# Last tokens of k and v on 128 partitions, token sums placed in VectorE's gaps, and another order of sigmoids, in a fused linear-attention and GEGLU kernel

## The chip, the cores and the metric

The kernel runs on one core of a Trainium2 chip. The metric is the device time of one execution in microseconds (us). Executions were timed on the chip, several for each kernel, and medians with their ranges are given. "Before" is the kernel as it was, "after" is the kernel with the whole change.

Names: PE is TensorE (matrix products), DVE is VectorE, ACT is ScalarE, POOL is GpSimd, SP is SyncE, which here only issues transfers. A letter q behind an engine's name is its sequencer. "Full clock" means that the throttle grants PE its full frequency.

## The reference, cut to what matters

```python
def _attn_ref(q, k, v, g_norm):            # q, k, v: (8 batches, 8 heads, 576 tokens, 64)
    kv  = np.einsum('bhsd,bhse->bhde', k, v)
    out = np.einsum('bhsd,bhde->bhse', q, kv)
    rms = np.sqrt(np.mean(out * out, axis=-1, keepdims=True) + 1e-06)
    return (out / rms * g_norm)

def _moe_ref(x, w_gate, w_val, w_out, w_res):   # x: 4608 tokens x 512, d_ff 1536
    g = x @ w_gate
    val = x @ w_val
    ffn_out = gelu(g) * val @ w_out              # (shortened)
    res_gate = 1.0 / (1.0 + np.exp(-(x @ w_res)))
    return x + res_gate * ffn_out
```

k^T v over all 576 tokens of a head has to be there before anything else can start: nothing of a batch's output exists without its last tokens.

## The kernel before

The tokens are worked on in nine blocks of 512. Blocks 0 to 7 hold the first 512 tokens of each batch, with four tokens (j = 0..3) of one head group on each partition; block 8 holds the 64 last tokens of every batch. Three places matter.

**The opening.** Batch 0's q, k and v come in halves (four heads first, then two head pairs one after the other), issued by SP. Its 64 last tokens of k and v are loaded apart, on 32 partitions with two tokens each, into tiles whose other 96 partitions are set to zero, so that their product may use all 128 rows:

```python
def load_first_last(half):
    hs = slice(half * HH, (half + 1) * HH)                    # four heads
    for i, t in enumerate((k, v)):
        nc.sync.dma_start(
            out=first_raw[i][half][0 : R // 2, :].rearrange("p (h x) -> p h x", h=HH),
            in_=t[0, hs, M0:S, :].rearrange("h (p j) d -> p h (j d)", j=2),
        )
...
for which, t in (("q", q), ("k", k), ("v", v)):
    load_first(which, t, 0, HH)
    if which == "k":
        load_first_last(0)
for pr in range(NP // 2, NP):                                 # head pairs 2 and 3
    load_first("q", q, 2 * pr, 2 * pr + 2)
    load_first("k", k, 2 * pr, 2 * pr + 2)
    if pr == NP // 2:
        load_first_last(1)
    load_first("v", v, 2 * pr, 2 * pr + 2)
...
def f_kv(pr):
    ...
    for j in range(NJ):
        nc.tensor.matmul(ps, lhsT=k16[:, j, cs], rhs=b16_t[0, "v"][:, hs, j * D : (j + 1) * D], ...)
    for j in range(2):
        kl, vl = (t[:, j].rearrange("p h d -> p (h d)")[:, cs] for t in first_last)
        nc.tensor.matmul(ps, lhsT=kl, rhs=vl, start=False, stop=(j == 1))
```

**The end of an ordinary block** (blocks 6 and 7 are the ones concerned). The output product is made of seven products of half size; bank A is written, read by DVE and written again. `rest` carries additions of tokens that the next block needs (`ts`):

```python
prod(w["A"], s_[1], wo_t[:, 1], False)
sub(nc.vector, w["F"], w["A"], w["d"], ALU.add)
prod(w["E"], a_of(blk, 1, 2), b_of(2, 1), False)
pf((0, 0), w["E"])
for f in rest:                       # all four token sums
    f()
prod(w["A"], s_[2], wo_t[:, 2], False)
c22 = res_all[part((1, 1))]
sub(nc.vector, c22, w["A"], w["d"], ALU.add)     # bank A is free only after this
prod(w["F"], s_[3], b_of(2, 2), False)
...
prod(w["A"], a_of(blk, 2, 2), wo_t[:, 3], False)
```

**The last block** makes its four sigmoids on ACT after two copies, in the order 2, 3, 0, 1; POOL then forms `u` from sigmoids 2 and 3, and DVE adds `u` near the end.

## Time and profile before

| | |
|---|---|
| time, median of the timed executions beside the change | 343.72 us (343.55 to 343.92, 4 runs) |
| the profiled execution | 348.22 us, of which 346.3 us from first to last instruction |
| busy: PE, DVE, ACT, POOL | 95%, 75%, 47%, 32% of that span |
| first product of the regular part (the first gps with four products in a row) | 27.31 us |

The page of the kernel before opens with these lines; the digits are the busy share in tenths, in 40 equal slices of the span:

```profile
span 346.3 us, 6525 instructions
...
PE   8779999999999999999999999999999899989992
```

PE is filled nearly everywhere. It is not in the first three slices (26 us: the opening), in two or three slices late in the run (the ends of blocks 6 and 7), and in the last (the tail). These are the places that the change touches. In the prediction and below, lines of the chain of waits read "start, duration, what", and lines of a timeline "start, duration, engine, line, operation, out<-in, shape, how often", with the idle time before it and its cause in brackets.

### The profile page before, as it was taken

The numbers are of one execution on the slowest core, as the hardware profiler recorded it, in microseconds if no ns is written. First come the engines' busy times: TensorE is split into PE (matmuls) and PEld (weight loads), VectorE is DVE, ScalarE is ACT, GpSimd is POOL, SyncE is SP. The second block draws the span as 40 slices with busy tenths as digits, with TensorE's granted clock in tenths as the row PEclk, the third lists the DMA queues.
The fourth block names the chain that finished last, engine by engine and source line by source line (L and its number), as shares of the span: only waits on it lengthen the run. The fifth ranks groups of instructions, "written<-read, shape, count | busy, mean of one in ns | idle before, by whom it ended". The sixth has DMA issues, their size and how long they took to land.

```text
span 346.3 us, 6525 instructions
## 1 busy us (share of the span) xinstructions
PE 330.3 (95%) x2576; PEld 202.9 (59%) x2576; DVE 258.3 (75%) x498; ACT 161.3 (47%) x289; POOL 110.1 (32%) x127
## 2 busy tenths in 40 slices
PE   8779999999999999999999999999999899989992
PEld 3534454444854476447644674466546778778882
DVE  5474529749958988878677978796799787677854
ACT  3355365454526361536163525353544366636750
POOL 2692160892043207400650066005000431151222
PEclk9999999999999999999999999999999999999999
DMA  7999999359389363983498349935103030011004
GB/s 242 281 182 204 194 203 169 86 132 182 44 148 180 122 77 107 188 94 70 140 172 87 61 123 178 105 61 139 62 0 61 2 137 2 2 51 73 0 2 121
DMA packets 76688, 38.82 MB, mean 112 GB/s; under 512 B 42098, under 2 KB 74354, under 8 KB 76658
## 3 DMA queue, kind: packets, MB, share of 16 engines
q0 software_dynamic: 38752, 17.17, 39.5%
q1 hardware_dynamic: 37328, 20.71, 22.0%
q10 hardware_dynamic: 578, 0.52, 0.4%
q8 instruction: 20, 0.33, 0.4%
q14 instruction: 10, 0.08, 0.1%
HBM read 38.80 MB, written 9.44 MB: 139 GB/s over the span
## 4 chain that ended last, share of the span: by engine, by line
PE 86%; DVE 7%; DMA 2%; ACT 2%; issue 1%; SPq 1%; DVEq 0%
PE gps L357 21%; PE vps L357 20%; PE wA L452 9%; PE rps L377 8%; PE Av L682 3%; PE Ag L682 3%; PE fps L394 3%; PE wD L452 3%; PE w L452 2%; DMA hid_s<-in_v_dram 2%; PE wF L452 2%; PE wE L452 2%; PE kvp L208 2%; PE Fv L682 2%; PE Fg L682 2%; DVE ts L425 1%
## 5 line engine op out<-in xcount | busy, mean ns | idle before, releaser
L345 ACT ACTIVATE ge<-gps 128x512 f16<-128x512 f32 x84 | 50.0, 597 | 98.5 <-PE gps L357 97.7
L357 PE MATMUL vps<-xT,wv 128*128 128x512 f16 x328 | 84.2, 379 | 0.8 <-DVE hid L346 0.8
L357 PE MATMUL gps<-xT,wg 128*128 128x512 f16 x328 | 84.3, 380 | 0.0
L346 DVE TENSOR_TENSOR hid<-ge,vps 128x512 f16<-128x512 f16 x84 | 57.4, 684 | 32.6 <-PE vps L357 28.7
L488 POOL TENSOR_TENSOR osb<-osb,t 128x512 f32<-128x512 f32 x28 | 36.2, 1311 | 138.9 <-DVE osb L484 133.1
L357 PEld LDWEIGHTS <-wv 128*128 128x128 f16 x328 | 32.1, 98 | 39.7 <-issue 1.1
L357 PEld LDWEIGHTS <-wg 128*128 128x128 f16 x328 | 30.7, 98 | 34.5 <-issue 0.2
L452 PEld LDWEIGHTS <-hid_s 128*128 128x128 f16 x384 | 37.6, 98 | 4.5 <-issue 0.2
L452 PEld LDWEIGHTS <-hid 128*128 128x128 f16 x288 | 28.1, 98 | 8.2 <-issue 3.5
L377 PE MATMUL rps<-wr,xT 128*128 128x512 f16 x144 | 32.5, 379 | 0.0
L386 ACT ACTIVATE th<-rps 128x512 f32<-128x512 f32 x36 | 21.5, 597 | 16.4 <-PE rps L377 16.4
L377 PEld LDWEIGHTS <-xT 128*128 128x128 f16 x144 | 14.1, 98 | 16.6
L245 DVE TENSOR_REDUCE ss<-sq 128x8 f32<-128x512 f32 x32 | 20.6, 680 | 2.9 <-ACT sq L243 2.7
L682 PEld LDWEIGHTS <-ws 128*128 128x128 f16 x192 | 18.8, 98 | 3.3 <-issue 1.2
L452 PE MATMUL wA<-wo_ts,hid_s 128*128 128x256 f16 x168 | 20.6, 273 | 0.0
L391 ACT ACTIVATE th<-th 128x512 f32<-128x512 f32 x36 | 19.8, 622 | 0.0
L303 DVE TENSOR_TENSOR t<-op,ny 128x512 f16<-128x512 f32 x28 | 17.9, 683 | 0.1
L243 ACT ACTIVATE sq<-op 128x512 f32<-128x512 f32 x28 | 15.3, 596 | 4.5 <-PE op L226 4.2
L317 DVE TENSOR_TENSOR t<-t,g 128x512 f16<-128x512 f16 x36 | 16.2, 500 | 0.1
L425 DVE TENSOR_TENSOR hid_s<-hid 128x1536 f16<-128x1536 f16 x16 | 15.3, 954 | 0.2
L719 POOL TENSOR_TENSOR hid<-ge,c 128x512 f16<-128x512 f16 x6 | 7.0, 1164 | 25.6 <-ACT ge L713 25.6
L452 PE MATMUL wA<-wo_ts,hid 128*128 128x256 f16 x84 | 10.3, 272 | 2.3 <-DVE osb L425 2.3
(172 smaller groups left out, 481.4 us busy)
## 6 DMA issues: line engine op xcount, KB each, us to landing
out_dram<-osb SPq DMA_DIRECT2D x14, 512.0 KB, 2.6
qraw<-in_q_dram POOLq DMA_DIRECT2D x7, 512.0 KB, 7.8
k<-in_k_dram POOLq DMA_DIRECT2D x7, 512.0 KB, 9.5
v<-in_v_dram POOLq DMA_DIRECT2D x7, 512.0 KB, 11.3
wg<-in_moe_w_gate_dram POOLq DMA_DIRECT2D x2, 512.0 KB, 8.6
wv<-in_moe_w_val_dram POOLq DMA_DIRECT2D x2, 512.0 KB, 9.4
wo<-in_moe_w_out_dram POOLq DMA_DIRECT2D x2, 512.0 KB, 14.2
out_dram<-osb SPq DMA_DIRECT2D x4, 256.0 KB, 2.8
```

What stands on the lines that cost most here:

```text
L245: nc.vector.tensor_reduce(out=out_, in_=sq, op=ALU.add, axis=mybir.AxisListType.X)
L303: nc.vector.tensor_tensor(out=t, in0=o, in1=scale, op=ALU.mult)
L345: nc.scalar.activation(out=ge, in_=gps, func=AF.Gelu)
L346: nc.vector.tensor_tensor(out=hids[blk][:, f, :], in0=ge, in1=vps, op=ALU.mult)
L357: nc.tensor.matmul(ps[:, j0 * P : j1 * P], lhsT=w[:, cc, :], rhs=xT_t[blk][:, j0:j1, cc, :], start=(cc == 0 and j0 == 0), stop=(cc == NP - ...
L377: nc.tensor.matmul(rps, lhsT=xT_t[blk][:, j, cc, :], rhs=wr16[:, cc, :], start=(cc == 0), stop=(cc == NP - 1),)
L386: nc.scalar.activation(out=th, in_=rps, func=AF.Tanh, scale=0.5)
L391: nc.scalar.activation(out=th, in_=th, func=AF.Copy, scale=0.5, bias=0.5)
L425: eng.tensor_tensor(out=out_, in0=in0, in1=in1, op=op)
L452: nc.tensor.matmul(ps[:, e - es[0], :], lhsT=a[:, f, e * P : (e + 1) * P], rhs=b[:, f, :], start=(start and e == es[0] and f == 0), stop=( ...
L488: nc.gpsimd.tensor_tensor(out=res_all[of], in0=res_all[of], in1=t_t[blk][of], op=ALU.add)
L682: nc.tensor.matmul(out_[:, r, :], lhsT=lhsT, rhs=rhs, start=(first and r == 0 and c == 0), stop=(c == 1), skip_group_check=True,)
```

## The change

Its intent: give the last tokens of batch 0 all 128 partitions (four heads of 32 rows each), so that loads and casts are short and no zeros are needed; place each token sum on its own in a gap of DVE, and the last tokens' normalisation in an earlier gap; start two sigmoids earlier in the last block. Cut to its core:

```diff
@@ the opening
-        first_last.append(t[:, 2 * H * NJ * D :][:, 0 : 2 * H * D].rearrange("p (j h d) -> p j h d", j=2, h=H))
-        first_raw.append([th_all[:, 2 * len(first_raw) + i, :] for i in range(2)])
+        first_last.append(t[:, 2 * H * NJ * D :][:, 0 : 4 * D].rearrange("p (i j d) -> p i j d", i=2, j=2))
+        first_raw.append([th_all[:, 2 * len(first_raw) + i, 0 : 2 * D] for i in range(2)])
...
-                out=first_raw[i][half][0 : R // 2, :].rearrange("p (h x) -> p h x", h=HH),
-                in_=t[0, hs, M0:S, :].rearrange("h (p j) d -> p h (j d)", j=2),
+                out=first_raw[i][half],
+                in_=t[0, hs, M0:S, :].rearrange("h (p j) d -> h p (j d)", j=2),
...
-    for t in first_last:
-        nc.vector.memset(t, 0.0)
...
+        for j in range(NJ - 1):
+            whole(j)                      # 128 rows, as before
         for j in range(2):
-            kl, vl = (t[:, j].rearrange("p h d -> p (h d)")[:, cs] for t in first_last)
-            nc.tensor.matmul(ps, lhsT=kl, rhs=vl, start=False, stop=(j == 1))
+            for e in range(2):            # 32 rows, one head
+                i = 2 * (pr % 2) + e
+                kl, vl = (t[i * R // 2 : (i + 1) * R // 2, pr // 2, j, :] for t in first_last)
+                nc.tensor.matmul(ps[halves(e), halves(e)], lhsT=kl, rhs=vl, start=False, stop=False)
+        whole(NJ - 1)
@@ the end of blocks 6 and 7
             prod(w["A"], s_[1], wo_t[:, 1], False)
+            aside("F")                    # the last tokens' normalisation (block 6)
             sub(nc.vector, w["F"], w["A"], w["d"], ALU.add)
+            aside("00")                   # one token sum
             prod(w["E"], a_of(blk, 1, 2), b_of(2, 1), False)
             pf((0, 0), w["E"])
-            for f in rest:
-                f()
+            aside("22")                   # one token sum
             prod(w["A"], s_[2], wo_t[:, 2], False)
             c22 = res_all[part((1, 1))]
             sub(nc.vector, c22, w["A"], w["d"], ALU.add)
+            aside("01")                   # one token sum
             prod(w["F"], s_[3], b_of(2, 2), False)
             ...
+            aside("11")                   # one token sum
@@ the last block
                 prod(wa[e], a_of(blk, 1, 1), b_of(1, 1), True, (e,))
+            for j in (2, 3):
+                m_sigmoid(j)
+            for e in range(2):
                 nc.scalar.copy(out=we[:, one[e], :], in_=wa[e])
             ...
-            for j in (2, 3, 0, 1):
+            for j in (0, 1):
                 m_sigmoid(j)
```

More of the change, by code (lines that the diff above doesn't have):

```diff
@@ L459, in prod, with out_by_products, aside @@
                 )
-    def out_by_products(blk, later, banks, rest=()):
+    def out_by_products(blk, later, banks, amid):
         w = {}
         s_ = hid_sums
+        def aside(ahead_of):
+            for f in amid.get(ahead_of, ()):
+                f()
         def res(jj):
@@ L870, in f_cast_last @@
     def f_cast_last(i, half, copy):
-        hs = slice(half * HH, (half + 1) * HH)
-        copy(
-            out=first_last[i].rearrange("p j h d -> p h j d")[0 : R // 2, hs, :, :],
-            in_=first_raw[i][half][0 : R // 2, :].rearrange("p (h j d) -> p h j d", h=HH, j=2),
-        )
+        copy(out=first_last[i][:, half], in_=first_raw[i][half].rearrange("p (j d) -> p j d", j=2))
     def f_qT(pr):
@@ L890, in f_kv, with whole @@
         hs, cs = of_pair(pr)
-        for j in range(NJ):
+        def whole(j):
             nc.tensor.matmul(
-                ps, lhsT=k16[:, j, cs], rhs=b16_t[0, "v"][:, hs, j * D : (j + 1) * D], start=(j == 0), stop=False
-            )
+                ps,
+                lhsT=k16[:, j, cs],
+                rhs=b16_t[0, "v"][:, hs, j * D : (j + 1) * D],
+                start=(j == 0),
+                stop=(j == NJ - 1),
+            )
+        for j in range(NJ - 1):
+            whole(j)
         for j in range(2):
-            kl, vl = (t[:, j].rearrange("p h d -> p (h d)")[:, cs] for t in first_last)
-            nc.tensor.matmul(ps, lhsT=kl, rhs=vl, start=False, stop=(j == 1))
+            for e in range(2):
[3 more added lines that the diff above has]
+        whole(NJ - 1)
     def f_kv_out(pr):
@@ L1084, in plan_attn @@
             if b == 3:
-                amid_out[m - 1] = [lambda: by_token(b), *begin]
+                amid_out[m - 1] = {"22": [lambda: by_token(b), *begin]}
             else:
@@ L1102, in plan_attn @@
             at(m, NF if b == 2 and j > 1 else n0 + j // 2, lambda j=j: a_t(b, j))
-        if rem:
-            at(m, NF + 3, lambda: a_t(b, NJ))
         for j in range(NJ):
@@ L1107, in plan_attn @@
         at(m, NF, lambda: d_xT(b, 0, NJ))
-        if rem:
-            at(m, NF + 3, lambda: a_x(b, NJ), lambda: d_xT(b, NJ, NJ + 1))
+        last = [lambda: a_t(b, NJ), lambda: a_x(b, NJ), lambda: d_xT(b, NJ, NJ + 1)]
+        if rem and b + 1 == B:
+            amid_out.setdefault(m, {})["F"] = last
+        elif rem:
+            at(m, NF + 3, *last)
     units = [(n, g) for g in range(NF // GF) for n in "gv"]
@@ L1170 @@
             if blk + 1 in LAST:
-                amid_out.setdefault(blk, []).extend(token_sums(blk + 1, nc.vector))
+                for ahead_of, f in zip(("00", "01", "22", "11"), token_sums(blk + 1, nc.vector)):
+                    amid_out.setdefault(blk, {}).setdefault(ahead_of, []).append(f)
             def products(blk=blk, outs=outs):
@@ L1179, in products @@
                 if blk < B:
-                    outs.extend(out_by_products(blk, blk == 1, out_at[blk], amid_out.get(blk, ())))
+                    outs.extend(out_by_products(blk, blk == 1, out_at[blk], amid_out.get(blk, {})))
                 else:
```

## The prediction

> **What bounds the kernel now.** I read the page first, then the chain of waits (it follows the last instruction back to what released it), and then, where the change touches that chain, the timeline of single engines. The page says who is busy:
>
> ```profile
> PE 330.3 (95%) x2576; PEld 202.9 (59%) x2576; DVE 258.3 (75%) x498; ACT 161.3 (47%) x289; POOL 110.1 (32%) x127
> PE 86%; DVE 7%; DMA 2%; ACT 2%; issue 1%; SPq 1%; DVEq 0%
> ```
>
> The second line is the chain by engine. TensorE (PE) carries 86% of it and the change takes no work from PE in the steady part, so only what stands in the other 14% can be won. VectorE (DVE) is on the chain in three places: the opening, the ends of blocks 6 and 7 (the last ordinary blocks, before those whose gate and value products use seven products), and the tail. The chain across the end of block 6, in order of time (start, us, what):
>
> ```profile
> 261.62 3.45 PE rps L377 x16
> ...
> 271.64 1.36 DVE ts L425 x2
> ...
> 273.16 0.41 DVE ts L425
> 273.57 0.61 DVE osb L425
> ...
> 274.23 1.47 PE wA L452 x12
> ...
> 279.27 0.70 DVE Fg L703
> ...
> 280.00 0.60 PE Ag L682 x4
> ```
>
> PE needs the bank wA free for its last product, but the DVE subtraction that reads it (osb<-wA,wd, the "c22" of the code) stands behind all four token sums (ts). Later DVE is late again, for Fg. The timeline of DVE shows why:
>
> ```profile
> 269.18 0.70 DVE L425 TENSOR_TENSOR wF<-wA,wd 128x512 f32<-128x512 f32 x1 [1.27 <-PE wA L452]
> ...
> 271.64 1.26 DVE L425 TENSOR_TENSOR ts<-xT,ts 128x512 f16<-128x512 f16 x1
> ...
> 276.41 1.63 DVE L303 TENSOR_TENSOR t<-o,ny 128x512 f16<-128x512 f32 x1
> ...
> 278.08 1.27 DVE L317 TENSOR_TENSOR t<-t,g 128x512 f16<-128x512 f16 x1
> ```
>
> One token sum takes 1.26 us instead of the 0.42 of its neighbours, and the last tokens' normalisation (t<-o,ny and t<-t,g) 1.63 + 1.27 us, while GpSimd (POOL) runs its 1.2 to 1.4 us additions. Earlier in the run the same two took 0.68 and 0.42 us with POOL out of the way. And DVE had sat idle 1.27 us before wF.
>
> The opening, by the chain and by bandwidth (40 slices of 0 to 14 us):
>
> ```profile
> 2.82 7.75 DMA hid_s<-in_v_dram
> ...
> 13.79 2.13 PE idle L842 x5
> ...
> 18.32 1.08 DVE v L863
> ```
> ```profile
> GB/s 0 0 0 0 1 82 79 266 366 369 375 380 389 345 356 331 272 212 170 243 348 360 370 385 372 356 304 168 205 205 266 375 388 376 243 328 360 369 380 383
> ```
>
> The first half of v lands at 10.57 us and PE starts k*v at 11.07, having run out of warming matmuls at 9.27. Bandwidth falls from some 375 to 170-250 GB/s twice, near 6-7 and 9.5-10.5 us, each time just behind a pair of the small transfers of the last tokens (32 partitions). The landing marks in the trace also show one straggler: 15 of the 16 increments for v come by 8.32 us, the last at 10.57.
>
> [...]a batch's k*v of 40 small tiled matmuls costs PE about 0.84 us with its entry and exit (242.30 to 243.14). [...]here full clock is first granted at 16.99 us, after the PE gap of 9.27 to 11.07.
>
> **Part 1, DVE in gaps.** The order of the built kernels shows for block 6: the last tokens' t<-o,ny and t<-t,g now stand before wF, and the four sums one each before pf(0,0), c22, pf(0,1), pf(1,1). Cost now, from the chain: from the start of rps to the end of the last wA, undisturbed block 5 takes 239.01-226.38 = 12.63 us, block 6 takes 275.70-261.62 = 14.08, block 7 takes 309.07-295.17 = 13.90. Excess 1.45 + 1.27 = 2.72. Then block 7's gate products: 295.17-275.70 = 19.47 against 327.42-309.07 = 18.35 for block 8, excess 1.12 (Fg). Sum 3.84 us, all on the PE chain.
> Does the new order fit? Before wF, DVE is idle 267.91 to 269.18; 0.68 + 0.42 = 1.10 fits, with POOL idle. The first sum follows wF at 269.88; its xT transpose landed at 268.63 by its marks; it ends before the sigmoid lets pf(0,0) start at 270.58. The second follows at once and starts before POOL's addition does, as the first does today. c22 then runs at about 271.8 to 272.5, and PE is busy with wF to 273.0: no stall. The two remaining sums may wait for POOL, but have PE's last product ahead of them. I book 3.7 of the 3.84 us.
>
> **Part 2, sigmoids in the last block.** ScalarE (ACT) does the same work. Two sigmoids (0.55 us each) go ahead of the copies of wA, whose last would end near 333.3, just before PE reuses wA at 333.5. pf(0) still waits for PE at 336.1, so the head gains nothing. But POOL starts u at about 334.15 instead of 335.24, and so is done with its last addition at about 339.35 instead of 339.97. The DVE addition of u, held by POOL today, then takes about 0.7 instead of this:
>
> ```profile
> 339.29 1.23 DVE L425 TENSOR_TENSOR osb<-osb,u 128x512 f32<-128x512 f32 x1
> ```
>
> Four DVE operations and the store follow in series. Gain 0.45 us.
>
> **Part 3, the opening.** Removed: two DVE memsets (about 1 us, off the chain) and 0.4 us from each of four casts (32x512 to 128x128), also mostly aside. Added: 16 small matmuls for 8[...]; three pairs lie on PE's path, so I book 0.5 us of loss. Moved: v. If four engines carry the small transfers, [...]the 0.5 us dip behind each pair should go. On four engines v would be done at about 8.5 us; with today's straggler of 2.2 us on one of the other twelve 9.2, on one of the four 10.5. PE's k*v then starts at 9.4 to 11.0 instead of 11.07, on average about 1.1 us earlier[...]. Against it: the v cast at 18.24, held by POOL's weight casts, which come when the weights land and move little. Net estimate 1.0 us, anywhere from -0.8 to +2.5.
>
> Sum: 3.7 + 0.45 + 1.0 = 5.15; 343.77 - 5.15 = 338.6 us.
>
> **Rivals.** (a) The opening gains nothing or loses, as k and v for the last two head pairs are late on four overloaded engines[...] or POOL's casts hold DVE anyway: 339.6 to 340.4. [...]Against it: the landings of the second part have about 3 us of slack (v's last part lands at 15.12, used at 18.24). (b) PE reaches full clock early and the opening gains 2.5 us or more: about 337. [...]Against it: the data of the second half then bounds. (c) [...]c22 is late by up to 1.2 us in both blocks: 341. Against it: c22 reads PSUM, and only one sum stands before it. (d) All of this off the path: 343.8; against it, the PE stalls are on the chain itself.
>
> **Range and chances.** The DVE part is read off stalls (3.3 to 3.9), the tail 0.2 to 0.6, the opening is the wide term. 336.6 to 340.6 should hold 8 in 10. Two per cent is 6.9 us and needs an opening gain over 2.6: one in ten. Slower by 2% would need a loss of 11 us in the opening: one in a hundred.
>
> **What would show it.** Right: no PE wait before the last wA of blocks 6 and 7 (spans 12.6 us), no wait for Fg (18.4 us), u's addition near 0.7 us; the dips behind the small transfers gone, v landed before 10 us, k*v before 10.5. Wrong: c22 behind a long ts; four landing marks late on every load; k*v at 11 or later; PE's first full-clock time unchanged and the first gps of the steady part still at 27.3.

## The result, and the profile after

After took 341.26 us (341.16 to 342.43, 4 runs) against 343.72 us (343.55 to 343.92, 4 runs) for before. The ratio is 0.9936, 95% interval 0.9914 to 0.9958: same within 2%, 2.5 us faster. A ratio here is the mean time of one kernel's runs over that of the other's of the same rounds, so it is not quite the ratio of the medians. Executions over 1.5% slower than the fastest of the same kernel are left out of the means. The prediction said 338.6 us, at most 340.6: it missed by 2.7 us, and its range by 0.7 us.

The page of after, the lines that answer to those of before:

```profile
span 339.4 us, 6537 instructions
...
PE 328.0 (97%) x2584; PEld 201.1 (59%) x2584; DVE 254.0 (75%) x496; ACT 161.3 (48%) x289; POOL 108.8 (32%) x127
...
PE   8779999999999899999999999999999999999993
...
PE 87%; DVE 7%; DMA 2%; SPq 2%; issue 1%; ACT 0%; POOL 0%; DVEq 0%; ACTq 0%
```

The holes of PE near the end of the run are filled. In the chain, ACT has gone and SPq, the issuing of transfers, has gone from 1% to 2%.

The chain of waits of after across the end of block 6:

```profile
259.32 3.45 PE rps L377 x16
...
268.08 1.31 PE wA L452 x12
269.39 1.31 PE wF L452 x12
270.70 1.31 PE wA L452 x12
272.01 0.44 PE Ag L692 x4
```

No wait of any other engine is left between rps and the last wA, which ends 272.01 - 259.32 = 12.69 us after rps began (14.08 before). Block 7 takes 302.97 - 290.35 = 12.62 us (13.90 before), and block 7's gate products 290.35 - 272.01 = 18.34 us (19.47 before). DVE's timeline shows why:

```profile
265.52 0.69 DVE L303 TENSOR_TENSOR t<-o,ny 128x512 f16<-128x512 f32 x1
266.24 0.42 DVE L317 TENSOR_TENSOR t<-t,g 128x512 f16<-128x512 f16 x1
...
267.48 0.42 DVE L425 TENSOR_TENSOR ts<-xT 128x512 f16<-128x512 f16 x1
...
269.48 0.69 DVE L425 TENSOR_TENSOR osb<-wA,wd 128x512 f32<-128x512 f32 x1 [0.18 <-issue]
```

The normalisation takes 0.69 + 0.42 us in place of 1.63 + 1.27, inside what had been an idle gap, and osb<-wA,wd (the c22 that frees bank A) is done at 270.17, before PE wants the bank at 270.70.

The opening is another matter. The chain of waits of after, in its first 26 us:

```profile
6.89 6.39 DMA hid_s<-in_v_dram
...
13.34 0.62 POOL v L871
...
14.00 0.33 PE kvp L897 x3
...
24.93 0.86 PE gps L357 x4
```

The transfer is the second part of v (head pair 2). It lands at 13.28, POOL casts it, PE makes k^T v with it, and some 11 us of dependent work later the regular part begins at 24.93. The landing marks of the trace (the increments of each transfer's semaphore) show how it lands: twelve of its sixteen by 10.78 us, the last four from 12.80 to 13.28. For the first half of v it is twelve by 8.24 and four at 8.95 to 9.37. Each of the new last-token loads has only four marks of landing (the first one at 6.74 to 7.22), where the old ones have sixteen in before. That a mark stands for one DMA engine is the author's reading. The packets of the trace agree with it: from 5.5 to 7.0 us, while the first two of these loads run, a median of 4 of their 512 B packets are in flight at a time, where it was 7 in before (5.0 to 6.0 us). A mark does not name an engine: the traces show how many lag, not which.

By the two profiles the change would gain 346.3 - 339.4 = 6.9 us, of which 27.31 - 24.93 = 2.4 us in the opening. By the timed executions it gains 2.5 us. What does not fit is before's profile: its execution took 348.22 us, 4.5 us more than the timed ones. So the opening has to be compared with another execution of before.

### The profile page after: what moved, and what is told of

Read it like the earlier page. It is cut to its first block, busy times and chain, and to the rows that moved or that the text cites. A ratio compares the mean times of both kernels' runs of the same rounds, so it can differ in the third digit from the quotient of the medians.

```text
span 339.4 us, 6537 instructions
## 1 busy us (share of the span) xinstructions
PE 328.0 (97%) x2584; PEld 201.1 (59%) x2584; DVE 254.0 (75%) x496; ACT 161.3 (48%) x289; POOL 108.8 (32%) x127
## 4 chain that ended last, share of the span: by engine, by line
PE 87%; DVE 7%; DMA 2%; SPq 2%; issue 1%; ACT 0%; POOL 0%; DVEq 0%; ACTq 0%
PE gps L357 19%; PE vps L357 19%; PE wA L452 11%; PE rps L377 8%; PE fps L394 3%; PE Av L692 3%; PE Ag L692 3%; PE wD L452 3%; PE wF L452 3%; PE wE L452 3%; PE w L452 2%; DMA hid_s<-in_v_dram 2%; PE kvp L208 2%; PE Fg L692 2%; PE Fv L692 2%; DVE hid L346 1%
## 5 line engine op out<-in xcount | busy, mean ns | idle before, releaser
L492 POOL TENSOR_TENSOR osb<-osb,t 128x512 f32<-128x512 f32 x28 | 35.3, 1276 | 138.3 <-DVE osb L488 132.4
L245 DVE TENSOR_REDUCE ss<-sq 128x8 f32<-128x512 f32 x32 | 20.6, 680 | 2.7 <-ACT sq L243 2.5
L452 PE MATMUL wA<-wo_ts,hid_s 128*128 128x256 f16 x168 | 20.6, 273 | 0.0
L317 DVE TENSOR_TENSOR t<-t,g 128x512 f16<-128x512 f16 x36 | 15.4, 479 | 0.1
L394 PE MATMUL fps<-wo,hid 128*128 128x512 f16 x48 | 11.2, 379 | 0.0
```

What stands on the lines that cost most here:

```text
L245: nc.vector.tensor_reduce(out=out_, in_=sq, op=ALU.add, axis=mybir.AxisListType.X)
L394: nc.tensor.matmul(fps, lhsT=hids[blk][:, f, j * P : (j + 1) * P], rhs=wo16[:, f, :], start=(f == 0), stop=(f == NF - 1))
L452: nc.tensor.matmul(ps[:, e - es[0], :], lhsT=a[:, f, e * P : (e + 1) * P], rhs=b[:, f, :], start=(start and e == es[0] and f == 0), stop=( ...
L492: nc.gpsimd.tensor_tensor(out=res_all[of], in0=res_all[of], in1=t_t[blk][of], op=ALU.add)
```

## The experiments

Every kernel below gave correct results. "Beside before" means timed on the same chip in the same rounds. Times are medians of all executions given.

### 1. Before once more

No edit.

> The kernel before, unchanged, profiled once more. Theory A (the profile of before was an atypical execution: it took 348.22 us where the timed ones took 343.7, and its opening had one DMA straggler and a late full clock): this profile has a span near 342 us instead of 346.3, the first half of v lands by about 8.5 us instead of 10.57 with no increment more than 0.5 us behind, full clock comes before 16.99 us, and the first steady gate product starts near 23 us instead of 27.3. Rival B (the profile was typical and profiling itself adds the 4 us): span again near 346, steady part again from 27.3.

Measured: 343.48 us in the one execution, the profiled one, with a span of 341.6 us; the eleven executions of before that were timed beside experiments 2 to 4 have the median 343.65 us. The chain of waits of this execution of before:

```profile
1.27 5.07 DMA kf<-in_k_dram
...
6.36 5.10 DMA hid_s<-in_v_dram
...
11.51 0.63 POOL v L863
...
12.18 0.38 PE kvp L892 x4
12.56 0.13 PE kvp L897 x2
...
22.68 0.86 PE gps L357 x4
```

v's first half has landed by 8.31 us on all sixteen marks, with no straggler, PE starts k^T v at 8.82, and the regular part begins at 22.68, not 27.31. The second part of v (head pair 2) lands at 11.46 and is cast at once: it has no slack at all. The chain's first line shows what holds back its issue: SP uses a load's semaphore again, and waits until the load that had it before, k's first half, has landed (6.34 us). Against this execution, after's regular part starts 24.93 - 22.68 = 2.25 us later. Before's first profile was an execution with a straggler, 4.6 us late from the opening on, and the opening was reasoned about from it. It was late in a second thing that the expectation names: full clock was granted to PE at 16.99 us there, and at 8.39 us here (9.68 in after).

### 2. The new sums and sigmoids with the old opening

```diff
 the change, without the hunks of the opening (loads, memsets, casts, f_kv stay as before)
```

> The DVE gaps and the sigmoid order, with the opening of before. Theory A: the DVE part is worth the 3.7 us and the tail the 0.5 us that the traces show, and the new opening costs the rest: 343.7 - 4.2 = 339.5 us, faster than the whole change by about 1.8. Rival B (the opening is neutral in timed runs and the DVE part is worth less than the traces say): 341.3. Rival C (the opening gains 2.4 us as the two profiles say and the DVE part nothing): 343.5.

Measured: 339.14 us (338.76 to 339.47, 4 runs) beside before at 343.65 (343.35 to 343.82, 11 runs); ratio 0.9869 (0.9856 to 0.9882). Two of the three parts of the change give 4.5 us, and the kernel beats both before and after. The regular part begins at 22.87.

### 3. The new opening alone

```diff
 the hunks of the opening only; sums and sigmoids stay as before
```

> Only the new opening. Theory A: it costs about 1.8 us, 345.5 us; landing marks of the small transfers 4 each. Rival B: 343.7. Rival C: 341.3.

Measured: 346.13 us (345.64 to 350.35, 6 runs); ratio 1.0098 (1.0061 to 1.0136). Its v lands as in after (second part: twelve marks by 10.59, four at 13.04 to 13.35), and the regular part begins at 25.01. The new opening loses 2.5 us by itself by the medians, and 2.1 us if the one execution of 350.35 is left out. With the new sums behind it, it loses much the same (341.26 for after against 339.14 in experiment 2, timed in other rounds).

### 4. After, with the last-token loads behind v

```diff
     load_first(which, t, 0, HH)
-    if which == "k":
+    if which == "v":
         load_first_last(0)
...
-        if pr == NP // 2:
-            load_first_last(1)
         load_first("v", v, 2 * pr, 2 * pr + 2)
+        if pr == NP // 2:
+            load_first_last(1)
```

> The whole change, but each pair of small transfers is queued behind the part of v instead of ahead of it. If four engines carrying 64 KB each are what delays v, v's first half lands by about 7.8 us on all engines and its second part by about 11.8 instead of 13.28, and the time falls by 1 to 1.8 us, to about 339.9. If not the order on the queue but the small products or their casts cost the time: 341.3, unchanged.

Measured: 341.63 us (340.82 to 345.84, 6 runs); ratio 0.9974 (0.9928 to 1.002). The best executions, 340.8 to 341.1, are 0.2 to 0.4 us below after, and two of six took over 345.5; the profile fell on one of these. The expected gain of 1 to 1.8 us did not come. In that profile v's first half landed whole by 7.34, and its second part at 11.30 (four late marks, the twelve others by 9.73), both about as early as was expected. But k^T v needs the last tokens too, and their loads now come last: those of v land at 9.32 and 13.26 us, as late as v itself did in after (9.37 and 13.28), and the chain of waits goes through the first of them. The order of the queue only changes what is late, and does not recover the loss. (PE lost its full clock between 20.6 and 27.5 us in this execution, so its later times are not compared.)

### 5. A four-engine source in the old layout, that failed to be one

```diff
-                in_=t[0, hs, M0:S, :].rearrange("h (p j) d -> p h (j d)", j=2),
+                in_=t[0, hs, M0:S, :].rearrange("h (a p j) d -> a p h (j d)", a=4, j=2),
```

> The kernel with the changed sums and sigmoids but the old opening (339.14 us), with one edit: the source of the last-token transfers is written with a slowest dimension of 4, same bytes, same places, same products. Theory T (the opening's loss is the transfer[...]): the marks for each of these loads fall to 4, v's second part lands on four engines some 2.3 us after the other twelve (13 us instead of 11.5), the steady gps starts near 24.9 instead of 22.7, and the time is 341.3 (ratio to before 0.993). Rival P (the loss is the small products, casts and mode changes): 339.1, steady gps at 22.7. If the marks stay at 16 the edit did nothing and the run says nothing.

Measured: 339.07 us (338.83 to 339.24, 4 runs) beside before at 343.55. The marks stayed at 16 for each load, so the edit did nothing and says nothing about engines. (The two outer dimensions run on without a break; that they were merged is the author's guess.) It serves as a repeat of experiment 2 on other rounds: 339.14 and 339.07 agree, and its regular part begins at 22.53.

### 6. The small products alone

```diff
 (experiment 2, and in f_kv, with the old tiles of 32 filled rows)
         for j in range(2):
-            kl, vl = (t[:, j].rearrange("p h d -> p (h d)")[:, cs] for t in first_last)
-            nc.tensor.matmul(ps, lhsT=kl, rhs=vl, start=False, stop=(j == 1))
+            for e in range(2):
+                kl, vl = (t[0 : R // 2, j, 2 * pr + e, :] for t in first_last)
+                nc.tensor.matmul(ps[halves(e), halves(e)], lhsT=kl, rhs=vl, start=False, stop=False)
+        whole(NJ - 1)
```

> The kernel with the changed sums and sigmoids but the old opening (339.14 us), with one edit: the last tokens' k*v is made of 16 products of 32 rows (two a token and head pair, between the whole ones) instead of 8 of 128 rows, as in the changed kernel; the transfers, casts and memsets are the old ones. Theory T: the products are off or nearly off the path, 339.1 to 339.6, steady gps at 22.7 to 23.2. Rival P: 340.5 to 341.3, steady gps at 24 to 25, and the k*v of a head pair visibly longer.

Measured: 339.61 us (339.34 to 344.17, 5 runs; four of them 339.34 to 339.62); ratio 0.9907 with the 344.17 in it. That is 0.5 us over the 339.07 of the same rounds. The chain of waits:

```profile
11.71 0.64 POOL v L873
...
12.39 0.33 PE kvp L902 x3
12.72 0.18 PE kvp L915 x4
12.90 0.18 PE kvp L902
...
23.33 0.86 PE gps L357 x4
```

k^T v of a head pair takes 0.33 + 0.18 + 0.18 us, against 0.38 + 0.13 in before. From the landing of v's second part (11.65) to the regular part it is 11.68 us; in before it was 22.68 - 11.46 = 11.22. The small products cost 0.46 us. Of this, 0.19 us lies in the products of head pair 2 (they end 1.42 us after the landing, against 1.23). The rest comes with a change of path: the chain of before goes on over DVE's cast of v's last part, that of this kernel over PE, with the last pair's products and 0.43 us of warming matmuls (products of zeros whose result nobody uses). What a change of the tiling mode itself costs was not measured.

### 7. The sums in gaps alone

```diff
 before, with only the hunks of the block ends (aside(...), the last tokens' normalisation)
```

> Before, with nothing but the sums and the last tokens' normalisation moved into DVE's gaps. By the prediction's first part this alone is worth 3.7 us: 343.65 - 3.7 = 339.95, ratio 0.989. If the parts add up, it lies 0.4 to 0.5 above the run with both (339.14), so 339.6. Rival: the two parts overlap and the sigmoids are worth nothing by themselves: 339.1.

Measured: 340.05 us (339.49 to 341.17, 6 runs); ratio 0.9895 (0.9874 to 0.9916): 3.5 us, as booked within the spread.

### 8. The last-token loads behind v, in the old opening

```diff
 experiment 2, with the diff of experiment 4
```

> The changed sums and sigmoids with the old opening (339.14 us), and the last-token loads of k and v queued behind v in each half instead of between k and v. v's first half should land about 0.9 us earlier (two issues of 0.45 us on SP before it), at 7.0 to 7.4 instead of 7.7 to 8.3. If the first landing of v sets the start of the steady part, gain of up to 0.9: 338.3. If the second part's data and POOL's casts set it (which I think likelier, PE has its warming matmuls to do until 8.8 anyway): 339.1, nothing. If the last-token casts come late: up to 340.

Measured: 340.87 us (340.33 to 345.08, 6 runs); ratio 0.995 (0.9903 to 0.9998). A miss: it is the third case in kind, but loses 1.7 us, twice what I had allowed for. k's second load of last tokens now lands at 11.51, behind v's second part (11.13), and its cast on POOL goes ahead of v's, so the regular part starts at 24.06 in the profiled execution. Two of six executions took 345 us. The old place of these loads, between k and v, was the right one.

### 9 and 10. Four more loads whose data nobody needs: tokens outermost, and heads outermost

The direct test of the transfer, without the new products and casts. To the kernel of experiment 2, each last-token load gets a second one of the same 64 KB, into a buffer that is not needed for tens of us:

```diff
+            nc.sync.dma_start(                                        # 9: the old way
+                out=res_all[0 : R // 2, 2 * i + half, :].rearrange("p (h x) -> p h x", h=HH),
+                in_=t[0, hs, M0:S, :].rearrange("h (p j) d -> p h (j d)", j=2),
+            )

+            nc.sync.dma_start(                                        # 10: the new way
+                out=res_all[:, 2 * i + half, 0 : 2 * D],
+                in_=t[0, hs, M0:S, :].rearrange("h (p j) d -> h p (j d)", j=2),
+            )
```

> Control for the next run. The kernel with the changed sums and sigmoids and the old opening (339.1 us), where each of the four last-token loads is followed by a second one of the same 64 KB, written the old way (32 tokens outermost[...]), to a buffer that nothing needs for tens of us. It costs two more issues of some 0.45 us on SP ahead of v in each half: v's first half about 0.9 us later (8.7 to 9.2 us). Time 339.5 to 340.5 under both theories.

> The same as the control with the same number of extra loads and the same bytes, but the extra ones written the new way (4 heads outermost, 128 partitions). Nobody waits for them. Theory T (four engines carry each of them, and the next v waits for those four): v's marks split into 12 early and 4 late, the four some 1.5 to 2.3 us behind in the second half, and the time is 1 to 2 us above the control's, 340.8 to 342. Rival P (casts and products of the new layout cost it, not the transfer): equal to the control within 0.3 us.

Measured: 340.94 us (340.16 to 341.2, 5 runs), ratio 0.9921 (0.9907 to 0.9935), with tokens outermost; 343.18 us (343.09 to 344.06, 5 runs), ratio 1.0 (0.9986 to 1.0014), with heads outermost. The same bytes in the same number of loads, needed by no product, cost 2.2 us more when written the new way, with the four heads as the outermost dimension of the source (and 128 partitions in place of 32 as the destination, which the edit changes with it). The chain of waits, tokens outermost and then heads outermost:

```profile
3.29 4.95 DMA osb<-in_v_dram
8.26 4.95 DMA hid_s<-in_v_dram
...
13.27 0.62 POOL v L877
...
24.43 0.86 PE gps L357 x4
```
```profile
3.60 5.45 DMA osb<-in_v_dram
9.07 6.22 DMA hid_s<-in_v_dram
...
15.34 0.62 POOL v L877
...
26.56 0.86 PE gps L357 x4
```

v's second part is issued 0.81 us later and takes 1.27 us longer; its first twelve marks are there by 12.04, its last four at 15.16 to 15.29. "Nobody waits for them" was not quite so: osb is the extra load's buffer, and in both runs SP waits until the first half's extra load of v has landed (8.24 and 9.05 us) before it issues v's second part, as that takes over its semaphore. So 0.81 of the 2.08 us of later landing passes through a wait that after does not have. The 1.27 us of longer transfer are the part that carries over: against experiment 1, v's second part in after takes 6.39 - 5.10 = 1.29 us longer, and is issued 0.53 us later. In both runs, the regular part begins 11.2 to 11.3 us after the landing of v's second part. (In the profiled execution of 10 PE also had half its clock from 12.75 to 16.16 us; the 11.27 us show that this was off the chain.) The control itself was 0.4 us above what I had expected: v's second part landed at 13.21 us, having waited for the extra load as told.

### 11. After once more

No edit.

> The changed kernel unedited, beside the two above. If 341.26 (4 runs) was typical: 340.9 to 341.6, with steady gps near 24.9 us. With the half us that the small products cost, the transfer's share under theory T is then 341.3 - 339.1 - 0.5 = 1.7 us, which is what the four-engine loads should cost over the control.

Measured: 341.45 us (341.3 to 342.3, 5 runs); ratio 0.9945 (0.9933 to 0.9958). After's first result was typical. v's second part lands at 13.50 us, again with four late marks, and the regular part starts at 25.15.

### 12. The sigmoids alone

```diff
 before, with only the hunks of the last block
```

> Before, with nothing but the sigmoids of the last block in the other order. The prediction's second part says 0.45 us: 343.1 (ratio 0.9987), and the addition of u in the tail at 0.7 us instead of 1.23. By the difference between the two kernels with and without it (340.05 and 339.1) it would be up to 0.9: 342.7. If it is worth nothing alone: 343.5.

Measured: 343.01 us (342.94 to 348.86, 5 runs) beside before at 343.50; ratio 0.9985 (0.9972 to 0.9999): 0.5 us. The 348.86, which was the profiled execution, again has an opening like that of before's first profile:

```profile
2.82 6.96 DMA hid_s<-in_v_dram
...
28.80 0.86 PE gps L357 x4
```

v's first half lands only at 9.78 us, with one mark behind the fifteen others (by 8.40), PE gets its full clock at 13.59 us and loses it again from 20.4 to 27.2, and the regular part begins at 28.80. I draw nothing else from this execution.

### The sums

The span splits into the start of the regular part and the rest, and the start into the landing of v's second part and what follows. Left out are the three profiles of long executions (before's first, and those of experiments 4 and 12) and experiment 8, whose chain goes through the last tokens of k and not through v (24.06 - 11.13 = 12.93 us):

| kernel | v's second part lands | regular part starts | difference | span | span less start |
|---|---|---|---|---|---|
| before again (1) | 11.46 | 22.68 | 11.22 | 341.6 | 318.9 |
| new opening alone (3) | 13.35 | 25.01 | 11.66 | 344.0 | 319.0 |
| sums alone (7) | 11.90 | 23.13 | 11.23 | 338.2 | 315.1 |
| sums and sigmoids (2) | 11.65 | 22.87 | 11.22 | 337.2 | 314.3 |
| the same again (5) | 11.32 | 22.53 | 11.21 | 336.9 | 314.4 |
| and small products (6) | 11.65 | 23.33 | 11.68 | 337.7 | 314.4 |
| and extra loads, tokens (9) | 13.21 | 24.43 | 11.22 | 339.2 | 314.8 |
| and extra loads, heads (10) | 15.29 | 26.56 | 11.27 | 341.3 | 314.7 |
| after | 13.28 | 24.93 | 11.65 | 339.4 | 314.5 |
| after again (11) | 13.50 | 25.15 | 11.65 | 339.6 | 314.5 |

In these profiles the fourth column has two values only: 11.2 with the old products, 11.7 with the small ones. The last has three: 319 without the sums, 315.1 with them, 314.3 to 314.8 with sigmoids too. What the new opening costs is thus 13.28 - 11.46 = 1.82 us of landing and 0.43 us of small products, 2.25 in all. (v's second part lands at 11.32 to 11.90 us in the five profiles of the old opening without extra loads, and at 13.28 to 13.50 in the three of the new one: the 1.82 us hold to some 0.4.) The rest gains 318.9 - 315.1 = 3.8 us with the sums, and 318.9 - 314.5 = 4.4 us with sums and sigmoids in after. 4.4 - 2.25 = 2.15 us; the medians say 2.46. The sums alone gain 3.5 us and the sigmoids alone 0.5, but both together 4.5 by the timed executions (experiments 2 and 5). This half microsecond is not explained; the executions of experiment 7 spread over 1.7 us.

## Why the prediction was wrong in its sum and right in two of its three parts

**Part 1, DVE in gaps: right, mechanism and size.** Booked 3.7 us; the profiles give 3.8 us, the timed executions 3.5. The stalls for wA and Fg are gone to the last tenth (12.69, 12.62 and 18.34 us where 12.6 and 18.4 were named), and c22 runs clear of PE: it took 0.69 us beside POOL's addition of 269.05 to 270.32. Three of the four sums of block 6 overlapped an addition of POOL's; the one that began while POOL was at work took 0.52 us, the others 0.42. The gating of the last part took 1.65 us behind POOL, but nothing on the chain waited for it.

**Part 2, sigmoids: right.** Booked 0.45 us, measured 0.49 us alone. DVE's timeline of after has the line that was asked for, u's addition at 0.69 us where it took 1.23:

```profile
333.19 0.69 DVE L425 TENSOR_TENSOR osb<-osb,u 128x512 f32<-128x512 f32 x1
```

In the kernel with the sums alone (experiment 7) it still takes 1.22 us.

**Part 3, the opening: wrong in sign.** "Net estimate 1.0 us", a gain; it is a loss of 2.25 us. Two steps of it failed: the time that it starts from, and the path.

The first is "PE's k*v then starts at 9.4 to 11.0 instead of 11.07, on average about 1.1 us earlier". The 9.4 to 11.0 came true: k*v started at 9.88 in after. The 11.07 us did not stand, as they came from the one execution in the profile, in which a straggler held the first half of v back to 10.57 us. That execution took 348.22 us and the timed ones 343.7, and both numbers lay before me: they do not differ by noise. In an ordinary execution v lands by 8.31 and k*v starts at 8.82, so k*v started 1.06 us later, not earlier.

The second is the path. The start of k*v was taken to set the start of the regular part, and rival (a) was set aside because "the landings of the second part have about 3 us of slack". That slack was read off the last part of v (landed at 15.12, used at 18.24) in the same late execution, in which DVE's cast of it took 1.16 us beside POOL's casts, and the first of v 0.43. In the ordinary one this part has 0.9 us (landed at 13.45, cast at 14.35), and the part before it, that of head pair 2, has none: the chain runs through it, and its lateness counts one for one (the table's fourth column). Rival (a) had named it: "k and v for the last two head pairs are late on four overloaded engines". In after, v's four late marks came 2.5 us behind the twelve (13.28 against 10.78). In before's profile most packets of the small loads took 27 ns, and in after the two last-token loads of a half land 0.94 to 0.99 us apart, mark for mark, some 30 ns for each of 32 packets (an estimate: 128 packets of 512 B a load, by four marks).

The 0.5 us booked as a loss for the small products was right as a sum, 0.43 to 0.46, though part of what was measured is the change of path told in experiment 6. The dips of bandwidth did not go either, as was hoped; here is after's row of 0 to 14 us, of 40 slices:

```profile
GB/s 0 0 0 0 1 76 164 255 334 290 348 380 383 369 345 309 361 363 307 296 236 315 366 278 173 146 135 231 379 356 373 215 236 228 274 290 278 339 339 319
```

The first of them, 135 to 173 GB/s near 9 us, fits engines that run dry while four are still behind from the small loads: the mean busy share of the engines falls to 4 tenths there, some 7 packets are in flight at a time from 8.5 to 9.5 us against 17 at 7.5 to 8.0, and v's first half has its last four marks at 8.95 to 9.37. The second, 215 to 290 GB/s from 10.9 to 12.9 us, has 7 to 9 tenths busy and is not explained.

That four engines carry each of the small loads was the author's assumption before any run showed it. The trace of after agrees: for the first load a mark right after the issue (2.91 us) and four at landing (6.74 to 7.22); a median of 4 of their packets in flight at a time; and in v behind them, four marks late in the first half (8.95 to 9.37, the twelve by 8.24) as in the second. Why v lags with them was not shown. That it is the same four engines, and that v's share on these stands behind the last tokens, is the author's reading; the marks do not name them. Experiments 9 and 10 show that the transfer alone costs it, with no new product or cast: 2.2 us, of which 1.27 us are v's own longer transfer.

Of the rivals, (a) happened, and more so than its 339.6 to 340.4 us said, since the loss was taken as at most 0.8 us. (b), (c) and (d) did not. The chance of 0.89 for "within 2%" was borne out, but rested on the size of the parts and not on this.

**What stays open.** Why some executions take 4 to 6 us more is not settled. It was seen in before's first profile, and in one of six executions of experiment 3, two of six in 4 and in 8, one of five in 6 and in 12. Three of these were profiled (before's first, 4 and 12). What the three share, by the trace's record of the granted clock, is a late clock: PE is first granted its full clock at 16.99, 13.80 and 13.59 us in them, and at 7.03 to 9.68 us in the eleven other profiles. A straggler in v's first half is in two of them only (in before's first, one mark at 10.57 and the fifteen others by 8.32; in 4 it landed whole by 7.34). No run tests whether the late clock is the cause, so of the 4.6 us in before's first profile it is not known how much is the straggler's. All of these are kernels of one core, on two chips (experiments 1 to 4 on one, 5 to 12 on another), too few to say which opening is prone to it. Nor is it tested whether the 128 partitions of the new destination play a part beside the heads of its source. What makes an issue longer is not shown either: SP's issue of v's second part took 1.52 us in after, and 0.39 in before again (experiment 1). And other ways to load the new layout have not been tried: one load for each head, for instance, would add issues on SP, each of some 0.45 us (0.37 to 0.51 in before's profile).

## What to carry to other kernels

Before reasoning about a stage from a profile, hold the profiled execution's own time against the timed ones: 348.2 against 343.7 meant that something in it was 4.5 us out of the ordinary, and the slack read in its opening was not there in an ordinary execution. A small load that is written with few heads outermost was not cheap here for being small: it landed with four marks instead of sixteen, and v, queued behind it, landed only with four late marks (in after, 2.5 us behind the twelve). And a change made of three parts is worth taking apart: here two of them without the third make 339.1 us, better than before and than the whole.
